# A third late weight set in the first phase, W2 casts ahead of negations, and low parts last in the second layer: a fused attention and expert kernel

## The chip, the cores and the metric

One Trainium2 chip, one core. The metric is the device time of one execution in microseconds (us). The engines are TensorE (PE; its weight loads PEld), VectorE (DVE), ScalarE (ACT), GpSimd (POOL) and SyncE (SP, which issues most DMAs). Each takes its instructions in the order of its own queue, and they wait for one another by semaphores.

## The reference

A linear attention with a complex decay over 768 steps, for 4 batches and 8 heads of 48 dimensions; its output, 3072 tokens of 384 features, goes through four experts of 1024 hidden units, whose outputs are summed with normalised weights. In float32:

```
mag   = sqrt(a_re**2 + a_im**2);  scale = minimum(mag, 0.999) / (mag + 1e-06)
a_re, a_im = a_re * scale, a_im * scale
for t in range(768):
    S_re, S_im = a_re[t]*S_re - a_im[t]*S_im + k[t] x v[t],  a_re[t]*S_im + a_im[t]*S_re
    y[t] = q[t] @ S_re
x = y, tokens by (heads * dims)                     # 3072 x 384
p = probs / (probs.sum(-1) + 1e-09)
out = sum over e of p[:, e] * (relu(x @ w1[e]) @ w2[e])
```

## The kernel before

Each large product keeps its float32 precision by splitting both operands into a high and a low part (names hh and hl, whi and wlo, xha and xla, shi and slo) and summing three matmuls: high by high, high by low, low by high. The high part is a copy by ScalarE into the matmul's own type, the low part the difference, by VectorE. For weights the low part is also made without VectorE: a DMA of GpSimd's queue casts the weights into the high part, ScalarE writes its negative into the low part's slot ("negation"), and a second DMA of GpSimd's queue adds the weights onto it.

**First phase (to line 925).** Twelve blocks g of 256 tokens. For each the decay, q and k are worked out on VectorE and ScalarE, the attention on TensorE (scores sc, L588, masked into scs by VectorE, L593; states G), and its output y goes to DRAM (y_d) and comes back as tokens xa. In between, for the block before, experts 0 and 1 run: eight steps f2 of two 128-wide parts u. `w1_step` makes the first layer's ph (18 matmuls, L234), hh (ScalarE, L244) and hl (VectorE, L245); `w2_step` multiplies hh and hl with the weights' second half, for each u and each of two token halves t: (hh, whi), (hh, wlo), (hl, whi), 12 matmuls on L254, into accumulators po. The order of all this is set by a scheduler, from the order in the program and the dependencies. The 16 weight parts of experts 0 and 1 lie in 16 slots each for high and low.

`check_all` and `late_weights(h)` are called ahead of the last block's steps. `late_weights` prepares a *weight set*: the first-layer weights of four of an expert's eight hidden parts, in the form that the second phase wants. It loads them raw (lw, four DMAs, L736), makes 15 sums and differences (`weight_sums`, lws and lwt, VectorE, L743), splits the 20 resulting 128 x 128 tiles by six copies on ScalarE (lwh, lwt, L749) and six subtractions on VectorE (lwl, lwm, L750), and writes both parts to DRAM (late_d, four DMAs on SP's queue, L753 and L754). lwl and lwm have one buffer each. Before, it is done for the two sets of expert 3.

**Second phase (L927 on).** Experts 2 and 3, over rounds R of 768 tokens, each with two units (h = 0 and 1, one weight set each). A unit takes 20 products of sums of tokens (X, parts xh and xl, by `prep_x` from Z, which is loaded from y_d) by the set's 20 tiles, 3 matmuls each (L935, into the accumulators pb0 to pb4), and the list UNIT says in which order they stand among copies to SN (C, by ScalarE), sums of accumulators (D, by VectorE), the hidden parts (H, L: hid) and *fills* F. A fill is a second-layer part `l2` of the unit before (matmuls on L935 into pob). For a set that is not in DRAM yet, `prep_w` loads the raw weights to free space (ACC, RX, SN), and makes the same sums and splits; a set in late_d is loaded by `fetch_w` straight into the slots (slots 0 to 4 for h = 0 of expert 2, 5 to 9 for h = 1, high and low, and a tile ext). Either way `second_w` takes the second-layer weights by casts (L1018), negations (L1020) and accumulating DMAs (L1022) into the slots 3, 4 or 8, 9. Slots become free as experts 0 and 1 finish on the last block.

What isn't TensorE's work in a unit waits in a list, `side`, in order; a B entry of UNIT takes so many of its items, and casts are taken as soon as they are first. Up to `held["on"]` the scheduler may still move the instructions; from there on they stay as written.

Names in the profile: lw0/lw1 are the two late sets, shi and slo the slots, SN the saved accumulators. L938 is any ScalarE copy of the second phase, L941 and L944 any VectorE sum of it, L947 GpSimd's.

Of the kernel before, what the change touches and what calls it, by code (L numbers as in the profile page):

```python
# [16 lines left out]
HD = H * D  # L17
# [104 lines left out]
def fast_path(ctx, tc, qkP, aP, vP, probsP, w, out, flag):  # L122
# [36 lines left out]
    late_d = [dram.tile([P, 2, len(WORDER) * P], F32, name=f"late_d{h}") for h in range(2)]  # L159
# [88 lines left out]
    def w2_step(f2, hh, hl, po):  # L248
        for u in range(2):
            i = 2 * f2 + u  # L250
            hi, lo = wts[i]
            for t in range(CG):
                for n, (ht, wt) in enumerate(((hh, hi), (hh, lo), (hl, hi))):
                    nc.tensor.matmul(po[t], ht[:, u, t * P:(t + 1) * P], wt[:, HD:],  # L254
                                     start=(i % FE == 0 and n == 0),
                                     stop=(i % FE == FE - 1 and n == 2))
# [28 lines left out]
    with ExitStack() as c1:  # L285
# [446 lines left out]
        def late_weights(h):  # L732
            i = (E1 + 1) * FE + 4 * h
            raw = big.tile([P, 4, NJ, P], F32, tag="A", name=f"lw{h}", bufs=NA)
            for u in range(4):
                nc.sync.dma_start(raw[:, u], w[i + u][:, :HD].rearrange("p (k c) -> p k c", k=NJ))  # L736
            s0, s1, h0 = (tmp(f"lw{nm}{h}").rearrange("p c (n x) -> p (c n) x", x=P) for nm in ("s", "t", "h"))
            l0 = big.tile([P, 12, P], F32, tag="qk", name=f"lwl{h}", bufs=1)
            l1 = big.tile([P, 12, P], F32, tag="K", name=f"lwm{h}", bufs=1)
# [11 lines left out]
            for c, (x, y) in enumerate(((h0, h1), (l0, l1))):  # L751
                d = late_d[h][:, c].rearrange("p (n x) -> p n x", x=P)
                nc.sync.dma_start(d[:, :12], x.bitcast(F32))  # L753
                nc.sync.dma_start(d[:, 12:], y[:, :8].bitcast(F32))  # L754
# [125 lines left out]
        for g in range(1, NG + 1):  # L880
            if g == NG:
                check_all()
                for h in range(2):
                    late_weights(h)
# [26 lines left out]
    with ExitStack() as c2:  # L911
# [141 lines left out]
        def fetch_w(e, h, base):  # L1053
            hi, lo, ext = places(e, h, base)
            for c, x in enumerate((hi, lo)):
                for n in range(3):
                    pin(nc.sync.dma_start(x[n].bitcast(F32), late_d[h][:, c, n * 2 * HD:(n + 1) * 2 * HD]))
                pin(nc.sync.dma_start(ext[:, c * 2 * P:(c + 1) * 2 * P].bitcast(F32), late_d[h][:, c, 6 * HD:]))
# [172 lines left out]
        jobs = [prep_w(E1, h, 5 * h, x[:, :half], y) for h, x, y in ((0, ACC, RX), (1, SN, SN[:, half:half + HD]))]  # L1231
# [3 lines left out]
        for job in jobs:  # L1235
            job[0]()
        side.pop(0)
        side += jobs[0][1] + jobs[0][2] + jobs[0][3] + jobs[1][1] + jobs[1][2]
# [232 lines left out]
```

## Time and profile before

| | |
|---|---|
| time, median of 3 executions | 981.32 us (980.24, 981.32, 983.77) |
| the profiled execution | 983.21 us |
| its span in the profile | 981.5 us |
| mean clock granted to TensorE | 0.994 |
| TensorE busy | 950.4 us of the span, 6717 matmuls |
| VectorE, ScalarE, GpSimd busy | 740.7, 479.2, 163.9 us |
| DMA | 134.32 MB, 137 GB/s over the span |

The span is what lies between the first and the last instruction; the execution's time includes some us around it. The first phase takes the span up to about 600 us, with the two phases overlapping from 564 us, when the first load of Z starts. Times inside the profile are counted from the start of the span. A timeline row gives start, length, engine, line, operation and tiles, with x3 for three of a kind in a row; in brackets stands how long the engine was idle before it, and what that was waiting for. Rows of tables by stretches give the window, then its length and the busy times of PE, PEld, DVE, ACT and POOL, each with the number of instructions, then PEclk, DMA share and GB/s.

### The profile page before, as it was taken

Reading aid. Unit: us, or ns where it says so; the run is one execution under the profiler, and the core shown is the slowest. Engines: PE = TensorE matmul, PEld = TensorE weight load, DVE = VectorE, ACT = ScalarE, POOL = GpSimd, SP = SyncE. Lnnn points to the kernel's source line nnn. Section 1 sums busy time; section 2 is a strip of 40 time slices with the busy share of each in tenths; the row PEclk is TensorE's granted clock in tenths of the full one; section 3 lists DMA queues with packets and bytes.
Section 4 is the critical chain, followed back from the end, with each engine's and each line's share of the span. In section 5 each row is a group of like instructions: output and inputs, shape, how many; then the busy total and the mean of one; then the engine's idle time right before and its main releaser. Section 6 shows DMA issues by size and latency. Waiting matters only on the chain.

```text
span 981.5 us, 17593 instructions
## 1 busy us (share of the span) xinstructions
PE 950.4 (97%) x6717; PEld 924.7 (94%) x6717; DVE 740.7 (75%) x1610; ACT 479.2 (49%) x952; POOL 163.9 (17%) x206
## 2 busy tenths in 40 slices
PE   5899998999999999999999999999999999999997
PEld 3799998999999999999999998999999999999997
DVE  7888989898888889878896286767675857576643
ACT  7755435355363636436263256545453545454430
POOL 6030000000000000000000007333533352323000
PEclk9999999999999999999999999999999999999999
DMA  9585276674756657393769159231513444131112
GB/s 300 182 158 158 57 194 141 158 152 147 175 138 157 157 134 177 123 226 107 169 162 296 49 177 293 57 97 49 137 66 113 162 124 112 49 99 49 49 49 76
DMA packets 110510, 134.32 MB, mean 137 GB/s; under 512 B 7824, under 2 KB 95424, under 8 KB 110416
## 3 DMA queue, kind: packets, MB, share of 16 engines
q1 hardware_dynamic: 98928, 106.17, 38.5%
q0 software_dynamic: 11488, 26.93, 11.7%
q8 instruction: 55, 0.90, 0.4%
q14 instruction: 39, 0.32, 0.1%
HBM read 87.20 MB, written 45.86 MB: 136 GB/s over the span
## 4 chain that ended last, share of the span: by engine, by line
PE 81%; DVE 6%; DMA 6%; ACT 4%; issue 1%; POOL 0%; SPq 0%; DVEq 0%; ACTq 0%; POOLq 0%
PE pob L935 20%; PE ph L234 17%; PE po L254 16%; PE pb L935 16%; PE sc L588 4%; PE dp L574 3%; PE yp L609 2%; PE yp L604 2%; PE ktp L556 1%; DMA y_d<-y 1%; DMA Kst<-k_d 1%; DMA shi<-w 1%; DMA xa<-y_d 1%; DMA wst<-w 1%; PE xp L639 1%
## 5 line engine op out<-in xcount | busy, mean ns | idle before, releaser
L935 PE MATMUL pob<-shi,hid 128*128 128x384 f32 x528 | 148.9, 336 | 0.7 <-DVE hid L944 0.6
L254 PE MATMUL po<-whi,hh 128*128 128x384 f32 x384 | 129.8, 339 | 1.1 <-ACT hh L244 1.1
L254 PE MATMUL po<-wlo,hh 128*128 128x384 f32 x384 | 129.1, 336 | 0.0
L254 PE MATMUL po<-whi,hl 128*128 128x384 f32 x384 | 124.6, 339 | 1.7 <-DVE hl L245 1.6
L244 ACT ACTIVATE hh<-ph 128x512 fp32r<-128x512 f32 x96 | 57.1, 595 | 140.5 <-PE ph L234 136.4
L947 POOL TENSOR_TENSOR Z<-Z 128x384 f32<-128x384 f32 x84 | 90.4, 1118 | 115.0 <-DVE xl L941 50.6
L234 PE MATMUL ph<-xha,whi 128*128 128x256 f32 x576 | 104.0, 287 | 1.2 <-ACT xha L221 1.2
L234 PE MATMUL ph<-xla,whi 128*128 128x256 f32 x576 | 101.1, 284 | 0.4 <-DVE xla L223 0.4
L234 PE MATMUL ph<-xha,wlo 128*128 128x256 f32 x576 | 101.3, 284 | 0.0
L935 PEld LDWEIGHTS pob<-shi,hid 128*128 128x128 f32 x528 | 96.5, 188 | 2.0 <-DVE hid L944 1.2
L935 PE MATMUL pb<-xh,shi 128*128 128x384 f32 x291 | 97.8, 338 | 0.3 <-DVE pb L941 0.2
L935 PE MATMUL pb<-xl,shi 128*128 128x384 f32 x288 | 97.0, 337 | 0.0
L935 PE MATMUL pb<-xh,slo 128*128 128x384 f32 x288 | 97.0, 337 | 0.0
L245 DVE SCALAR_TENSOR_TENSOR hl<-ph,hh 128x512 fp32r<-128x512 f32 x96 | 65.9, 687 | 35.4 <-ACT hh L244 34.8
L935 PE MATMUL pob<-slo,hid 128*128 128x384 f32 x264 | 88.4, 335 | 0.0
L234 PEld LDWEIGHTS ph<-xha,whi 128*128 128x128 f32 x576 | 85.9, 190 | 2.5 <-ACT xha L221 1.5
L234 PEld LDWEIGHTS ph<-xla,whi 128*128 128x128 f32 x576 | 82.6, 191 | 0.6 <-DVE xla L223 0.6
L234 PEld LDWEIGHTS ph<-xha,wlo 128*128 128x128 f32 x576 | 82.8, 190 | 0.2 <-issue 0.2
L938 ACT ACTIVATE SN<-pb 128x384 f32<-128x384 f32 x96 | 47.1, 492 | 65.7 <-PE pb L935 58.2
L941 DVE TENSOR_TENSOR xl<-Z,xh 128x384 fp32r<-128x384 f32 x104 | 59.9, 606 | 21.5 <-ACT xh L938 13.6
L938 ACT ACTIVATE hid<-pb 128x384 fp32r<-128x384 f32 x76 | 37.2, 490 | 75.9 <-PE pb L935 75.5
L254 PEld LDWEIGHTS po<-whi,hl 128*128 128x128 f32 x384 | 70.8, 188 | 3.3 <-DVE hl L245 3.2
(232 smaller groups left out, 2098.5 us busy)
## 6 DMA issues: line engine op xcount, KB each, us to landing
qk<-qkP SPq DMA_DIRECT2D x24, 384.0 KB, 7.1
acc_d<-acc POOLq DMA_DIRECT2D x24, 384.0 KB, 5.1
ACC<-acc_d SPq DMA_DIRECT2D x48, 192.0 KB, 3.2
A<-aP SPq DMA_DIRECT2D x22, 384.0 KB, 8.2
Z<-y_d SPq DMA_DIRECT2D x16, 384.0 KB, 3.8
q_d<-Q SPq DMA_DIRECT2D x12, 387.0 KB, 4.0
Qst<-q_d SPq DMA_DIRECT2D x12, 387.0 KB, 6.0
v<-vP SPq DMA_DIRECT2D x24, 192.0 KB, 2.7
```

The source lines that it names most:

```text
L234: ins = nc.tensor.matmul(ph[:, u, :], wt[:, j * P:(j + 1) * P], xt[:, j, :], start=(n == 0), stop=(n == 3 * NJ - 1))
L244: wts["hh"] = nc.scalar.activation(hh, ph, AF.Relu)
L245: nc.vector.scalar_tensor_tensor(hl, ph, 0.0, hh, op0=ALU.max, op1=ALU.subtract)
L254: nc.tensor.matmul(po[t], ht[:, u, t * P:(t + 1) * P], wt[:, HD:], start=(i % FE == 0 and n == 0), stop=(i % FE == FE - 1 and n == 2))
L574: ins = nc.tensor.matmul(d_ps[:, h, :], KT[:, h, :], vc[:, h * D:(h + 1) * D], start=True, stop=True)
L588: ins = nc.tensor.matmul(s_ps[:, h, :], Kc[:, hf * 4 + h, :], Qc[:, hf * 4 + h, :], start=True, stop=True)
L604: ins = nc.tensor.matmul(yo, st[:, o:o + n], Qc[:, o // D, :], start=True, stop=False)
L609: ins = nc.tensor.matmul(yo, vc[:, o:o + n], sc[h // 4][:, h % 4, :], start=first, stop=True)
L935: return tc.keep_in_program_order(nc.tensor.matmul(*args, **kw))
L938: return pin(nc.scalar.activation(dst, src, fn, scale=scale))
L941: pin(nc.vector.tensor_tensor(dst, x, y, op=op))
L947: nc.gpsimd.tensor_tensor(dst, x, y, op=op)
```

## The change

Four edits:

- `late_weights` is called for three sets, (expert 2, h = 0), (expert 3, h = 0) and (expert 3, h = 1); the first of them is new. The second phase then fetches this set with `fetch_w` and no longer loads, sums and splits it; `prep_w` remains for (expert 2, h = 1).
- In `side` both sets' casts of second-layer weights come first, then the first set's negations, then the sums of the second. The negations of slots 8 and 9 (`late`) come in the first unit behind a gap of four, with one token sum ahead of them.
- `w2_step` takes all eight products of hh first, for both u and t, and then the four of hl.
- In unit 1 the fill that is left empty is the sixth and no longer the eighth.

```diff
--- before.py
+++ after.py
@@ -156,7 +156,8 @@
     y_d = [dram.tile([HD, G], F32, name=f"y_d{g}") for g in range(NG)]
     acc_d = [dram.tile([P, CG, HD], F32, name=f"acc_d{g}") for g in range(NG)]
 
-    late_d = [dram.tile([P, 2, len(WORDER) * P], F32, name=f"late_d{h}") for h in range(2)]
+    late_d = {(e, h): dram.tile([P, 2, len(WORDER) * P], F32, name=f"late_d{e}_{h}")
+              for e, h in ((E1, 0), (E1 + 1, 0), (E1 + 1, 1))}
 
     wts = {}
     whi = {}
@@ -246,14 +247,14 @@
         return hh, hl
 
     def w2_step(f2, hh, hl, po):
-        for u in range(2):
-            i = 2 * f2 + u
-            hi, lo = wts[i]
-            for t in range(CG):
-                for n, (ht, wt) in enumerate(((hh, hi), (hh, lo), (hl, hi))):
-                    nc.tensor.matmul(po[t], ht[:, u, t * P:(t + 1) * P], wt[:, HD:],
-                                     start=(i % FE == 0 and n == 0),
-                                     stop=(i % FE == FE - 1 and n == 2))
+        for part in ((hh, (0, 1)), (hl, (0,))):
+            for u in range(2):
+                i = 2 * f2 + u
+                for t in range(CG):
+                    for n in part[1]:
+                        nc.tensor.matmul(po[t], part[0][:, u, t * P:(t + 1) * P], wts[i][n][:, HD:],
+                                         start=(i % FE == 0 and part[0] is hh and n == 0),
+                                         stop=(i % FE == FE - 1 and part[0] is hl))
 
     class MoE:
         def __init__(self):
@@ -729,14 +730,14 @@
             nc.tensor.matmul(n_ps, good, one1, start=True, stop=True)
             nc.vector.tensor_scalar(flag, n_ps, float(P), None, op0=ALU.is_lt)
 
-        def late_weights(h):
-            i = (E1 + 1) * FE + 4 * h
-            raw = big.tile([P, 4, NJ, P], F32, tag="A", name=f"lw{h}", bufs=NA)
+        def late_weights(e, h):
+            i = e * FE + 4 * h
+            raw = big.tile([P, 4, NJ, P], F32, tag="A", name=f"lw{i}", bufs=NA)
             for u in range(4):
                 nc.sync.dma_start(raw[:, u], w[i + u][:, :HD].rearrange("p (k c) -> p k c", k=NJ))
-            s0, s1, h0 = (tmp(f"lw{nm}{h}").rearrange("p c (n x) -> p (c n) x", x=P) for nm in ("s", "t", "h"))
-            l0 = big.tile([P, 12, P], F32, tag="qk", name=f"lwl{h}", bufs=1)
-            l1 = big.tile([P, 12, P], F32, tag="K", name=f"lwm{h}", bufs=1)
+            s0, s1, h0 = (tmp(f"lw{nm}{i}").rearrange("p c (n x) -> p (c n) x", x=P) for nm in ("s", "t", "h"))
+            l0 = big.tile([P, 12, P], F32, tag="qk", name=f"lwl{i}", bufs=1)
+            l1 = big.tile([P, 12, P], F32, tag="K", name=f"lwm{i}", bufs=1)
             rows, last_ = raw[:, :3], raw[:, 3]
             for ops in weight_sums((s0, s1), rows, last_):
                 for o in ops:
@@ -749,7 +750,7 @@
                 nc.scalar.activation(hi, src, AF.Copy)
                 nc.vector.tensor_tensor(lo, src, hi, op=ALU.subtract)
             for c, (x, y) in enumerate(((h0, h1), (l0, l1))):
-                d = late_d[h][:, c].rearrange("p (n x) -> p n x", x=P)
+                d = late_d[e, h][:, c].rearrange("p (n x) -> p n x", x=P)
                 nc.sync.dma_start(d[:, :12], x.bitcast(F32))
                 nc.sync.dma_start(d[:, 12:], y[:, :8].bitcast(F32))
 
@@ -880,8 +881,8 @@
         for g in range(1, NG + 1):
             if g == NG:
                 check_all()
-                for h in range(2):
-                    late_weights(h)
+                for e, h in late_d:
+                    late_weights(e, h)
             first = FIRST.get(g, 2)
             end = first + len(MORE) - 1
 
@@ -1054,8 +1055,8 @@
             hi, lo, ext = places(e, h, base)
             for c, x in enumerate((hi, lo)):
                 for n in range(3):
-                    pin(nc.sync.dma_start(x[n].bitcast(F32), late_d[h][:, c, n * 2 * HD:(n + 1) * 2 * HD]))
-                pin(nc.sync.dma_start(ext[:, c * 2 * P:(c + 1) * 2 * P].bitcast(F32), late_d[h][:, c, 6 * HD:]))
+                    pin(nc.sync.dma_start(x[n].bitcast(F32), late_d[e, h][:, c, n * 2 * HD:(n + 1) * 2 * HD]))
+                pin(nc.sync.dma_start(ext[:, c * 2 * P:(c + 1) * 2 * P].bitcast(F32), late_d[e, h][:, c, 6 * HD:]))
             ready.add(("w", e, h))
             return second_w(e, h)
 
@@ -1228,14 +1229,14 @@
                     bg(op[1])
 
         half = C2 * HD
-        jobs = [prep_w(E1, h, 5 * h, x[:, :half], y) for h, x, y in ((0, ACC, RX), (1, SN, SN[:, half:half + HD]))]
+        casts, rests = fetch_w(E1, 0, 0)
+        loads, sums, more, late = prep_w(E1, 1, 5, ACC[:, :half], RX)
         freed.update(range(16))
         side += prep_x(0)
         side[0][2]()
-        for job in jobs:
-            job[0]()
+        loads()
         side.pop(0)
-        side += jobs[0][1] + jobs[0][2] + jobs[0][3] + jobs[1][1] + jobs[1][2]
+        side += casts + more + rests + sums
         drain()
         held["on"] = True
         todo_x = []
@@ -1250,8 +1251,8 @@
                     side += todo_x[:1]
                     tail = []
                     if R == 0:
-                        side += [["gap", None, 2, None]] + jobs[1][3] + [["gap", None, 2, None]]
-                    if R in (1, NB2):
+                        side += todo_x[1:2] + [["gap", None, 4, None]] + late
+                    elif R in (1, NB2):
                         casts, tail = fetch_w(E1 + 1, *((0, 10) if R == 1 else (1, 0)))
                         side += todo_x[1:2] + [["gap", None, 3, None]] + casts
                     else:
@@ -1268,7 +1269,7 @@
                 def fill(k, u=2 * R + h):
                     if u == 0 and k == 0:
                         mo.flush()
-                    elif u > 1 or (u, k) == (0, 6) or (u == 1 and k < FE - 1):
+                    elif u > 1 or (u, k) == (0, 6) or (u == 1 and k != 5):
                         l2()
 
                 unit(R, h, fill)
```

Lines of the program behind the first edit are one higher than before: L245 becomes L246, L750 L751, L938 L939, L1018 L1019.

In the rows below, in the order in which an engine takes them, the brackets name whose semaphores a row waits for: an engine, or a DMA queue (DMAHW for SP's, DMASW for GpSimd's).

**VectorE, end of the late sets, ahead of the last block's first scores.** Before (lw1 is the last set, hl10_1 the hidden low part that TensorE's step of block 10 waits for, scs11 masked scores of block 11):

```order
L750 TENSOR_TENSOR lwl1_6535<-lws1_6532,lwh1_6534 128x768 [waits DMAHW4_49,Activation_49]
L750 TENSOR_TENSOR lwm1_6536<-lw1_6527,lwt1_6533 128x256 [waits DMAHW7_49]
L581 TENSOR_TENSOR G11_0_6175<-G10_1_5906,dp11_0_6166 112x384 [waits PE_49]
L750 TENSOR_TENSOR lwm1_6536<-lw1_6527,lwt1_6533 128x128
L750 TENSOR_TENSOR lwm1_6536<-lw1_6527,lwt1_6533 128x256
L750 TENSOR_TENSOR lwm1_6536<-lwt1_6533 128x384
L750 TENSOR_TENSOR lwl1_6535<-lws1_6532,lwh1_6534 128x768 [waits Activation_49]
L245 SCALAR_TENSOR_TENSOR hl10_1_6136<-ph10_1_6116,hh10_1_6135 128x512 [waits Activation_49]
L593 TENSOR_TENSOR scs11_0_0_6182<-sc11_0_0_6177,maskp_140 128x512 [waits PE_49]
L593 TENSOR_TENSOR scs11_0_1_6189<-sc11_0_1_6184,maskp_140 128x512 [waits PE_49]
```

After, the same place, where lw24 and lw28 are the second and the third set:

```order
L751 TENSOR_TENSOR lwl24_6536<-lws24_6533,lwh24_6535 128x768 [waits DMAHW4_49,Activation_49]
L751 TENSOR_TENSOR lwm24_6537<-lw24_6528,lwt24_6534 128x256 [waits DMAHW0_49]
L751 TENSOR_TENSOR lwm24_6537<-lw24_6528,lwt24_6534 128x128
L751 TENSOR_TENSOR lwm24_6537<-lw24_6528,lwt24_6534 128x256
L751 TENSOR_TENSOR lwm24_6537<-lwt24_6534 128x384
L751 TENSOR_TENSOR lwl24_6536<-lws24_6533,lwh24_6535 128x768 [waits Activation_49]
L744 TENSOR_TENSOR lws28_6574<-lw28_6569 128x384 [waits DMAHW7_49,DMAHW2_49,DMAHW1_49]
L744 TENSOR_TENSOR lws28_6574<-lw28_6569 128x128
L744 TENSOR_TENSOR lws28_6574<-lw28_6569 128x128 [waits DMAHW3_49]
L744 TENSOR_TENSOR lws28_6574<-lw28_6569 128x256
L744 TENSOR_TENSOR lws28_6574<-lw28_6569 128x128
L744 TENSOR_TENSOR lwt28_6575<-lw28_6569 128x128 [waits DVE_49]
```
```order
L582 TENSOR_TENSOR G11_0_6176<-G10_1_5907,dp11_0_6167 112x384 [waits PE_49]
L744 TENSOR_TENSOR lwt28_6575<-lw28_6569 128x128 x2
L246 SCALAR_TENSOR_TENSOR hl10_1_6137<-ph10_1_6117,hh10_1_6136 128x512 [waits Activation_49]
L744 TENSOR_TENSOR lws28_6574<-lws28_6574,lw28_6569 128x256 [waits DVE_49]
L744 TENSOR_TENSOR lws28_6574<-lws28_6574 128x256 [waits DVE_49]
L594 TENSOR_TENSOR scs11_0_0_6183<-sc11_0_0_6178,maskp_141 128x512 [waits PE_49]
```

The wait for the first set's write (lwm1, lwm24) stays; behind it six sums of the third set, waiting for its loads, now stand ahead of G11_0, and two more ahead of hl10_1.

**ScalarE, in the first unit.** slo8 and slo9 are negations, SN copies of accumulators, hid hidden parts. Before:

```order
L938 ACTIVATE hid0_7128<-pb3_7115 128x384 [waits PE_49]
L938 ACTIVATE SN_6894<-pb1_7081 128x384 [waits PE_49]
L938 ACTIVATE slo8_6948<-shi8_6943 128x384 [waits DMASW1_49]
L938 ACTIVATE slo8_6948<-shi8_6943 128x384 [waits DMASW2_49]
L938 ACTIVATE slo9_6949<-shi9_6944 128x384 [waits DMASW3_49]
L938 ACTIVATE hid1_7144<-pb4_7118 128x384 [waits PE_49]
L938 ACTIVATE SN_6894<-pb0_7077 128x384 [waits PE_49]
L938 ACTIVATE SN_6894<-pb1_7081 128x384 [waits PE_49]
L938 ACTIVATE slo9_6949<-shi9_6944 128x384 [waits DMASW4_49]
L938 ACTIVATE SN_6894<-pb0_7077 128x384 [waits DVE_49,PE_49]
```

After:

```order
L939 ACTIVATE hid0_7152<-pb3_7139 128x384 [waits PE_49]
L939 ACTIVATE SN_6936<-pb1_7100 128x384 [waits PE_49]
L939 ACTIVATE hid1_7162<-pb4_7142 128x384 [waits PE_49]
L939 ACTIVATE SN_6936<-pb0_7096 128x384 [waits PE_49]
L939 ACTIVATE SN_6936<-pb1_7100 128x384 [waits PE_49]
L939 ACTIVATE SN_6936<-pb0_7096 128x384 [waits DVE_49,PE_49]
L939 ACTIVATE slo8_6998<-shi8_6993 128x384 [waits DMASW4_49]
L939 ACTIVATE slo8_6998<-shi8_6993 128x384 [waits DMASW5_49]
L939 ACTIVATE hid2_7198<-pb3_7139 128x384 [waits PE_49]
L939 ACTIVATE shi15_7206<-SN_6936 128x384 [waits DVE_49]
```

The negations moved from ahead of hid1 and three copies to SN to behind them.

**GpSimd's queue, start of the second phase.** DMA rows with shi are casts, those with slo accumulations. Before:

```order
L1018 DMA shi3_6932<-w 128x384 [waits DMASW1_49,PE_49]
L1018 DMA shi3_6932<-w 128x384
L1018 DMA shi4_6933<-w 128x384 [waits DMASW3_49,PE_49]
L1018 DMA shi4_6933<-w 128x384
L1022 DMA slo3_6937<-w 128x384 [waits DMASW5_49,Activation_49]
L1022 DMA slo3_6937<-w 128x384 [waits Activation_49]
L1022 DMA slo4_6938<-w 128x384 [waits DMASW7_49,Activation_49]
L1022 DMA slo4_6938<-w 128x384 [waits DMASW0_49,Activation_49]
L947 TENSOR_TENSOR Z_6893<-Z_6893 128x384 [waits DMAHW3_49,DMAHW4_49,DMAHW2_49,DMAHW5_49,DMAHW1_49,DMAHW6_49,DMAHW0_49,DMAHW7_49,DVE_49,Pool_49]
L1018 DMA shi8_6943<-w 128x384 [waits DMASW1_49,PE_49]
L1018 DMA shi8_6943<-w 128x384 [waits DMASW2_49]
```

After:

```order
L1019 DMA shi3_6974<-w 128x384 [waits PE_49]
L1019 DMA shi3_6974<-w 128x384 [waits DMASW1_49]
L1019 DMA shi4_6975<-w 128x384 [waits PE_49]
L1019 DMA shi4_6975<-w 128x384 [waits DMASW3_49]
L1019 DMA shi8_6993<-w 128x384 [waits PE_49]
L1019 DMA shi8_6993<-w 128x384 [waits DMASW5_49]
L1023 DMA slo3_6979<-w 128x384 [waits Activation_49]
L1023 DMA slo3_6979<-w 128x384 [waits DMASW7_49,Activation_49]
L1019 DMA shi9_6994<-w 128x384 [waits DMASW0_49,PE_49]
L1019 DMA shi9_6994<-w 128x384 [waits DMASW1_49]
L1023 DMA slo4_6980<-w 128x384 [waits DMASW2_49,Activation_49]
```

The casts of shi8 and shi9 moved ahead of the first token sum (Z), in between those of slo3 and slo4.

## The prediction

> **What bounds the kernel now.** The page's head and its table of busy times come first, then TensorE's waits.
>
> ```profile
> span 981.5 us, 17593 instructions
> PE 950.4 (97%) x6717; PEld 924.7 (94%) x6717; DVE 740.7 (75%) x1610; ACT 479.2 (49%) x952; POOL 163.9 (17%) x206
> ```
> ```profile
> PE lp L202 <- DMA wst<-w: 9.6, 1, 9.6
> PE qp L446 <- DVE Q L486: 2.5, 1, 2.5
> PE pb L935 <- ACT SN L938: 2.1, 1, 2.1
> PE po L254 <- DVE hl L245: 1.6, 3, 0.7
> ...
> PE kp L565 <- ACT KT L557: 0.6, 1, 0.6
> PE pob L935 <- DVE hid L944: 0.6, 1, 0.6
> ```
>
> TensorE works for 950.4 of 981.5 us, so 31.1 us of idling is all that an order can win at an unchanged clock. The change alters no matmul's shape and no count of them, so I look only at where TensorE stops, or runs slowly. In the waits (engine, line, what was waited for: total, times, longest) the first two rows, 12.1 us, are the kernel's start, which the change leaves alone. The four below lie where it moves something.
>
> The three waits of the second layer are these, in TensorE's timeline (start, length, work, in brackets the idle time before and its releaser):
>
> ```profile
> 205.68 0.44 PE L254 MATMUL po<-whi,hl 128*128 128x384 f32 x1 [0.46 <-DVE hl L245]
> 431.12 0.44 PE L254 MATMUL po<-whi,hl 128*128 128x384 f32 x1 [0.42 <-DVE hl L245]
> 576.59 0.62 PE L254 MATMUL po<-whi,hl 128*128 128x384 f32 x2 [0.75 <-DVE hl L245]
> ```
>
> The longest stop of the second phase, and what ScalarE did then:
>
> ```profile
> 610.87 0.62 PE L935 MATMUL pb<-xh,ext 128*128 128x384 f32 x2 [2.07 <-ACT SN L938]
> ```
> ```profile
> 608.02 0.53 ACT L938 ACTIVATE slo<-shi 128x384 fp32r<-128x384 f32 x1 [0.89 <-DMA shi<-w]
> 609.54 0.52 ACT L938 ACTIVATE slo<-shi 128x384 fp32r<-128x384 f32 x1 [0.99 <-DMA shi<-w]
> 609.97 0.47 ACT L938 ACTIVATE hid<-pb 128x384 fp32r<-128x384 f32 x1
> 610.34 0.86 ACT L938 ACTIVATE SN<-pb 128x384 f32<-128x384 f32 x2
> ```
>
> ScalarE takes its instructions in order. Three negations (slo<-shi) stand ahead of hid and the SN copies, and two of them wait for casts of W2 that GpSimd issued only here:
>
> ```profile
> 588.59 2.16 POOL L1018 DMA_DIRECT2D shi<-w  x4
> 600.79 2.22 POOL L1018 DMA_DIRECT2D shi<-w  x4
> ```
>
> The SN copies free the accumulators that TensorE wants next, so it stops for 2.07 us. That is not all it costs. The table by stretches shows the clock right behind the stop (PEclk, the last column but two):
>
> ```profile
> 612.00:613.00 1.00, 1.00 (x5) 0.98 (x4) 0.69 (x2) 0.19 (x1) 0.90 (x2) 0.50 1.09 201
> 613.00:614.00 1.00, 1.00 (x5) 1.00 (x5) 0.55 (x2) 0.49 (x1) 1.00 (x3) 0.50 1.17 202
> 614.00:615.00 1.00, 1.00 (x5) 1.00 (x5) 1.00 (x3) 0.16 (x1) 1.00 (x3) 0.50 1.15 198
> 615.00:616.00 1.00, 1.00 (x6) 1.00 (x5) 0.89 (x3) 0.74 (x2) 0.12 (x1) 0.80 1.15 198
> ```
>
> Three us at half the clock and one at 0.80 lose 3 x 0.5 + 0.2 = 1.7 us. I read this as the price of the stop, so that it goes with the stop.
>
> The Trainium skill, "TensorE: Matmul & The Clock Gate", Part 1, has the gate go to half speed after an idle window of about 3.4 us, in windows that run freely. By that rule a stop of 2.07 us can't do it, and the slow stretch would stay: 1.7 us less gain. The stretch's length, 3 to 4 us, agrees with one such window; what started it does not, and where the two differ I go by the trace.
>
> **The low parts last.** A step of the second layer is 12 matmuls. Before, hl is read by the third of them, now by the ninth, so VectorE gets six matmuls more. What such a place costs, and what follows on it:
>
> ```profile
> 534.75 0.34 PE L254 MATMUL po<-whi,hh 128*128 128x384 f32 x1
> 534.93 0.34 PE L254 MATMUL po<-wlo,hh 128*128 128x384 f32 x1
> ```
>
> They start 0.18 us apart, so six give 1.1 us, more than the longest wait of 0.75. All three go: -1.6 us (0.46 + 0.42 + 0.75). The reordering itself costs nothing, for the same instructions stand in the same step.
>
> The scheduler also rearranges a little around blocks 0 to 1 (82 to 95 us): KT's copies on ScalarE now stand behind a logarithm and an exponential of the next group. The nearest row is the existing wait for KT, 0.6 us: it can go (-0.6), or grow by one or two such activations (+1.5). I take +0.5.
>
> **The transition.** In the changed order the casts of weights 8 and 9 stand in GpSimd's queue right behind those of 3 and 4, ahead of its first Z sum. They start where the last reader of those slots in the first phase ends, not at 600.79:
>
> ```profile
> 591.25 0.34 PE L254 MATMUL po<-whi,hl 128*128 128x384 f32 x1
> ```
>
> The old ones were waited for until 609.5, 8.7 us behind the first issue; from 592 on, the same gives about 601. The negations now stand behind hid1 and the SN copies, and would start near 607. So both causes go: no SN copy stands behind a negation that waits. -2.1 us for the stop, and -1.7 for the clock. Who waits for the later negations: GpSimd's accumulation of slo8 and slo9, then their reads in unit 2, over 10 us on.
>
> The fetched set comes by eight DMAs of 2.6 MB (six of 128 x 768 floats, two of 128 x 256), in place of four raw loads, 15 sums and six splits. Those sums were VectorE's work up to 600, where TensorE does not wait for it, so their absence wins nothing by itself. But two small loads of ext now go ahead of the Z loads on SP's queue, for which VectorE waits already:
>
> ```profile
> 571.62 1.50 DVE L941 TENSOR_TENSOR Z<-Z 128x384 f32<-128x384 f32 x3 [1.49 <-DMA Z<-y_d]
> ...
> 575.85 0.68 DVE L245 SCALAR_TENSOR_TENSOR hl<-ph,hh 128x512 fp32r<-128x512 f32 x1
> ```
> ```profile
> 574.98 0.34 PE L254 MATMUL po<-whi,hh 128*128 128x384 f32 x1
> ```
>
> One subtraction (0.5) has moved from ahead of this hl to behind it, so it would end at 576.0 if Z comes as before, and at 576.9 if Z comes 0.9 us later, two issues. The ninth matmul wants it at 574.98 + 8 x 0.18 = 576.4. I put 0.2 us on this (0 to 0.5).
>
> The wait for hid is 0.60 us:
>
> ```profile
> 635.86 0.62 PE L935 MATMUL pob<-shi,hid 128*128 128x384 f32 x2 [0.60 <-DVE hid L944]
> ```
>
> VectorE's rows there are the same as before, only with less ahead of them. Between 0 and 0.6 I take 0.3.
>
> **The third late set.** What it adds on VectorE is read from the two that are there, the sums by their group (count, busy time) and the end of the second set by the timeline:
>
> ```profile
> L743 DVE TENSOR_TENSOR lws<-lw 128x128 f32<-128x128 f32 (+2 forms) x10 | 3.2, 365 | 0.1
> ```
> ```profile
> 528.90 0.42 DVE L750 TENSOR_TENSOR lwm<-lw,lwt 128x256 fp32r<-128x256 f32 x1 [1.51 <-DMA late_d<-lwm]
> 529.25 0.55 DVE L581 TENSOR_TENSOR G<-G,dp 112x384 f32<-112x384 f32 x1
> ...
> 530.72 0.95 DVE L750 TENSOR_TENSOR lwl<-lws,lwh 128x768 fp32r<-128x768 f32 x1
> 531.59 0.68 DVE L245 SCALAR_TENSOR_TENSOR hl<-ph,hh 128x512 fp32r<-128x512 f32 x1
> ```
>
> The second set's last part starts at 528.90, when the first set's lwm has been written out (its buffer is the only one). Now the first group of subtractions waits for the same write, and behind it stand lwl, six sums of the third set, G11_0 and two more sums, and only then hl10_1. One load of the third set is issued ahead of that write, so I let the wait end at 530.3, 1.4 us later. From there, by these rows: four lwm 1.4 (528.90 to 530.72 without G), lwl 0.9, six sums 1.7 (five are half of the 3.2, one more is about 0.3, and neighbours overlap a little), G11_0 0.5, two sums 0.4, hl 0.7: 535.9. The ninth matmul wants it at 534.75 + 8 x 0.18 = 536.2. So hl10_1 comes just in time; with its third matmul wanting it, at 535.1, it would be 0.8 us late. Of the two masked scores scs11_0 behind it each comes some tenths later than before; between 0 and 2.5 us lie open here, by what these rows can slip, and I take 0.5, since the sum above ends just in time. What speaks for a small price is the empty time behind: in the table by stretches VectorE (third column of busy times) is free from there on, and so are the DMA queues (last column but one).
>
> ```profile
> 520.00:530.00 10.00, 10.00 (x79) 10.00 (x78) 8.38 (x27) 5.65 (x11) 0.85 (x1) 1.00 1.08 329
> 530.00:540.00 10.00, 10.00 (x93) 9.56 (x92) 4.18 (x7) 1.59 (x3) 0.00 (x0) 1.00 0.67 211
> 540.00:550.00 10.00, 10.00 (x94) 9.56 (x93) 2.07 (x3) 3.36 (x9) 0.00 (x0) 1.00 0.12 29
> ```
>
> **The sum.** -1.6 (hl) - 2.1 (stop) - 1.7 (clock) - 0.3 (hid) + 0.5 (block 0 to 1) + 0.2 (Z) + 0.5 (late set) = -4.5 us. The profiled execution took 983.21 us, which gives 978.7; against the median of the three runs, 981.32 (the profiled one is 1.9 above it), 976.8. About 0.5%, 4.9 us, is what a measurement of this kernel can tell from no change, so the forecast lies just at that edge.
>
> **Rivals.**
>
> *Everything gained, nothing paid.* Without the three costs and with the whole of hid: -1.6 - 2.1 - 1.7 - 0.6 = -6.0, 975.3. For it speak VectorE's empty rows behind 530; against it the order of ScalarE at 82 us. Chance 0.2.
>
> *The stop moves.* The copy that TensorE waits for also waits for VectorE in the changed order, and for its own place behind the other work. If another wait holds SN as long, the 2.1 and 1.7 stay: -1.6 - 0.3 + 1.2 = -0.7, 980.6. For it: DMA share is still 1.1 in the rows from 612 to 616, so the casts can land late again. Against it: they are issued 8 to 9 us sooner. Chance 0.2.
>
> *The slow stretch is not the stop's.* Then 1.7 stay: -2.8, 978.5. (The rule of the Trainium skill's "TensorE: Matmul & The Clock Gate", Part 1, told above, gives the same.) For it: the DMA queues are full in the same four rows, so something else than the stop is special there. Against it: it begins 1 us behind the stop's end. Chance 0.1.
>
> *Slower: the late set holds VectorE.* The DMA share was 1.08 already from 520 to 530; the third set adds 0.8 MB of loads and 2.6 MB of writes there, some 10 us of the queues at the 329 GB/s of that row. If the loads land at 540 rather than by 532.6, where the sums are ready for them, the six sums, hl10_1 and scs11 wait in VectorE's queue: hl10_1 would be ready near 543.3, 7 us late, and such a stop would bring a slow stretch (1.7) too. -4.5 - 0.5 + 7.1 + 1.7 = +3.8, 985.1. It decides from a stop of about 3.3 us (3.3 + 1.7 = 5.0), which is loads landing behind 536. Against it: the share falls to 0.67 in the ten us behind. Chance 0.1.
>
> **How the numbers follow.** The forecast has 0.4, with 974.8 to 978.5 as its own range, by the bounds of its costs. Below 976.4 (faster by over 0.5%) lie the first rival and half of the forecast: 0.4. Slower by over 0.5% is the last: 0.1. The rest, 0.5, is within. The range leaves out the last rival and the lowest tail of the first: 974.0 to 982.0.
>
> **What would show it.** The waits list without hl; no stop near 610 and PEclk 1.00 from 608 to 620; in VectorE's timeline the subtraction behind the write near 530, and hl10_1 by 536; TensorE without a stop at 535 to 546; KT's wait near 92. A stop over 3 us between 534 and 548, or one near 610 with another releaser, would make the prediction wrong.

## The result and the profile after

The changed kernel takes 976.15 us (median of 6 executions, 974.47 to 977.94), the kernel before, run beside it, 983.03 (980.24 to 987.04). The ratio is 0.9931, with a 95% interval of 0.9906 to 0.9956: 0.69% faster, 0.44 to 0.94. The profiled execution took 977.62 us with a span of 975.8, which is 5.7 us less than the span of before, where 4.5 was forecast; the medians lie 6.9 us apart.

The head of the page after, and TensorE's waits (engine, line, what was waited for: total, times, longest); each line number is one higher than before:

```profile
span 975.8 us, 17612 instructions
...
PE 946.6 (97%) x6717; PEld 923.2 (95%) x6717; DVE 740.7 (76%) x1610; ACT 479.2 (49%) x952; POOL 165.0 (17%) x206
```
```profile
PE pb L936 <- DVE pb L942: 1.2, 2, 1.0
...
PE po L255 <- DVE hl L246: 0.9, 1, 0.9
PE kp L566 <- ACT KT L558: 0.7, 1, 0.7
PE pob L936 <- DVE hid L945: 0.5, 1, 0.5
```

The row "pb <- ACT SN" is gone. Of the three waits for hl one is left, 0.9 us, and there is a new one of 1.0 for a sum of VectorE. Something does not add up at first: the waits fell by little (TensorE idled for 31.1 us of the span before, for 975.8 - 946.6 = 29.2 now), and still the span is 5.7 us shorter, since the *busy* time fell by 3.8 with the same matmuls: about 1.5 of it is the slow stretch of before, and for the rest see e7 and e8.

Where the time went is seen best by matmuls: the start of the n-th matmul of either trace, set against the n-th of the other. So far ahead is the changed kernel:

| n | before, at us | ahead by, us |
|---|---|---|
| 240 | 51.7 | 0.5 |
| 1440 | 203.0 | 0.1 |
| 1680 | 233.4 | 1.3 |
| 3240 | 426.5 | 1.7 |
| 3960 | 515.5 | 2.4 |
| 4320 | 560.1 | 2.2 |
| 4560 | 595.4 | 2.4 |
| 4680 | 619.3 | 4.9 |
| 4920 | 663.1 | 6.0 |

Behind 663 us nothing moves any more. So 2.4 us come from the first phase, 2.6 from the first unit, where the long stop was, and 1.1 from unit 2 near 634 to 645 (the time axis of before).

GpSimd's queue after, the casts that were at 588.59 and 600.79:

```profile
576.53 1.13 POOL L1019 DMA_DIRECT2D shi<-w  x2 [5.76 <-PE po L255]
580.45 2.13 POOL L1019 DMA_DIRECT2D shi<-w  x4 [2.79 <-PE po L255]
...
584.69 1.23 POOL L1019 DMA_DIRECT2D shi<-w  x2
```

All eight are issued by 586, where the prediction had those of slots 8 and 9 start from 592 on: the slots come free sooner than it read.

ScalarE, then VectorE, then TensorE at the place of the old stop:

```profile
607.49 0.93 ACT L939 ACTIVATE slo<-shi 128x384 fp32r<-128x384 f32 x2
...
610.31 0.92 ACT L939 ACTIVATE slo<-shi 128x384 fp32r<-128x384 f32 x2
611.14 0.47 ACT L939 ACTIVATE slo<-pb 128x384 fp32r<-128x384 f32 x1
```
```profile
611.64 0.56 DVE L945 SCALAR_TENSOR_TENSOR slo<-pb,slo 128x384 fp32r<-128x384 f32 x1 [0.64 <-ACT slo L939]
612.12 0.56 DVE L942 TENSOR_TENSOR pb<-pb,SN 128x384 f32<-128x384 f32 x1
```
```profile
612.73 0.44 PE L936 MATMUL pb<-xh,shi 128*128 128x384 f32 x1 [0.98 <-DVE pb L942]
```

The negations no longer wait for a DMA. But two of them, at 610.31, stand ahead of a copy (slo15) that VectorE waits for, and behind that stands the sum that TensorE needs: the stop is shorter and has another cause. The table by stretches (window; length and busy times of PE, PEld, DVE, ACT, POOL; PEclk; DMA share; GB/s) shows that no slow clock follows it:

```profile
612.00:613.00 1.00, 0.27 (x1) 0.28 (x2) 1.00 (x3) 0.27 (x1) 1.00 (x3) 1.00 0.75 131
613.00:616.00 3.00, 3.00 (x19) 3.00 (x19) 2.17 (x5) 1.84 (x4) 1.52 (x3) 1.00 1.08 225
```

The hl that is still waited for, in VectorE's and TensorE's timeline:

```profile
570.76 1.50 DVE L942 TENSOR_TENSOR Z<-Z 128x384 f32<-128x384 f32 x3 [1.01 <-DMA Z<-y_d]
...
574.52 0.68 DVE L246 SCALAR_TENSOR_TENSOR hl<-ph,hh 128x512 fp32r<-128x512 f32 x1
```
```profile
575.26 0.62 PE L255 MATMUL po<-whi,hl 128*128 128x384 f32 x2 [0.85 <-DVE hl L246]
```

TensorE is here 2.2 us earlier than before, but Z is only 0.9 us earlier (570.76, before 571.62): its loads, and the two of ext now ahead of them, do not follow TensorE's gain. The length of this wait is not fixed: in five executions of this order (the changed kernel, e7, e4, the changed kernel's later run f1, and e8) the starts there lie 1.19, 1.37, 1.06, 0.67 and 0.40 us apart. And the late set, with VectorE's rows and the hl matmuls:

```profile
528.02 0.96 DVE L751 TENSOR_TENSOR lwm<-lw,lwt 128x256 fp32r<-128x256 f32 x3 [3.72 <-DMA late_d<-lwm]
...
530.24 1.49 DVE L744 TENSOR_TENSOR lws<-lw 128x384 f32<-128x384 f32 x5
...
532.72 0.68 DVE L246 SCALAR_TENSOR_TENSOR hl<-ph,hh 128x512 fp32r<-128x512 f32 x1
```
```profile
533.67 0.87 PE L255 MATMUL po<-whi,hl 128*128 128x384 f32 x4
```

hl10_1 is ready at 533.4, 0.3 us before its first reader, as forecast, and the sums did not wait for their loads.

### The profile page after: what moved, and what is told of

It reads as the page before. It is cut to its first block, busy times and chain, and to the rows that moved or that the text cites. A ratio compares the mean times of both kernels' runs of the same rounds, so it can differ in the third digit from the quotient of the medians.

```text
span 975.8 us, 17612 instructions
## 1 busy us (share of the span) xinstructions
PE 946.6 (97%) x6717; PEld 923.2 (95%) x6717; DVE 740.7 (76%) x1610; ACT 479.2 (49%) x952; POOL 165.0 (17%) x206
## 4 chain that ended last, share of the span: by engine, by line
PE 84%; DVE 5%; DMA 4%; ACT 3%; issue 1%; SPq 0%; DVEq 0%; ACTq 0%
PE pob L936 20%; PE ph L235 18%; PE po L255 17%; PE pb L936 16%; PE sc L589 4%; PE dp L575 3%; PE yp L610 2%; PE yp L605 2%; DMA k_d<-K 1%; PE ktp L557 1%; DMA lw<-w 1%; DMA Kst<-k_d 1%; PE xp L640 1%; DVE xl L942 1%; DVE lws L744 1%
## 5 line engine op out<-in xcount | busy, mean ns | idle before, releaser
L245 ACT ACTIVATE hh<-ph 128x512 fp32r<-128x512 f32 x96 | 57.1, 594 | 135.4 <-PE ph L235 134.8
L246 DVE SCALAR_TENSOR_TENSOR hl<-ph,hh 128x512 fp32r<-128x512 f32 x96 | 65.9, 687 | 35.3 <-ACT hh L245 34.6
L255 PE MATMUL po<-whi,hl 128*128 128x384 f32 x384 | 84.9, 337 | 0.9 <-DVE hl L246 0.9
L939 ACT ACTIVATE SN<-pb 128x384 f32<-128x384 f32 x96 | 47.3, 492 | 67.1 <-PE pb L936 59.8
L255 PEld LDWEIGHTS po<-whi,hh 128*128 128x128 f32 x384 | 72.4, 189 | 1.5 <-ACT hh L245 1.5
L939 ACT ACTIVATE hid<-pb 128x384 fp32r<-128x384 f32 x76 | 37.3, 490 | 72.2 <-PE pb L936 71.8
```

The lines of the kernel that those rows point to most:

```text
L245: wts["hh"] = nc.scalar.activation(hh, ph, AF.Relu)
L246: nc.vector.scalar_tensor_tensor(hl, ph, 0.0, hh, op0=ALU.max, op1=ALU.subtract)
L255: nc.tensor.matmul(po[t], part[0][:, u, t * P:(t + 1) * P], wts[i][n][:, HD:], start=(i % FE == 0 and part[0] is hh and n == 0), stop=(i % ...
L939: return pin(nc.scalar.activation(dst, src, fn, scale=scale))
```

## The experiments

All but e7, which was only profiled, were timed against the kernel before on the same chip. "Ahead" is read as in the table above, from the profiled execution.

| run | what it is | median, us | ratio to before (95%) | span, us |
|---|---|---|---|---|
| e1 | before, low parts last | 980.49 | 0.9973 (0.9950 to 0.9995) | 981.1 |
| e3 | before, casts first | 979.27 | 0.9965 (0.9942 to 0.9988) | 977.3 |
| e9 | before, third set made but unused | 982.87 | 1.0000 (0.9985 to 1.0014) | 977.9 |
| e2 | changed, low parts mixed | 978.67 | 0.9967 (0.9956 to 0.9978) | 975.7 |
| e8 | changed, eighth fill empty | 977.24 | 0.9937 (0.9915 to 0.9959) | 975.6 |
| e4 | changed, negations early | 976.20 | 0.9932 (0.9909 to 0.9956) | 975.3 |
| e6 | e4, and Z loaded first | 975.37 | 0.9922 (0.9892 to 0.9952) | 973.4 |
| e10 | before, low last, casts first, negations early | 975.28 | 0.9935 (0.9922 to 0.9948) | 972.7 |
| e11 | e10, sixth fill empty | 974.30 | 0.9910 (0.9886 to 0.9934) | 972.8 |

Spans alone differ by a us or so from one execution to the next, at the start and at the loads of the first phase's scores (L588); so a run's argument rests on its rows, and these are of one execution. That of e1 was the longest of its ten (982.80 us), those of e9 and e10 were the shortest of their ten and six.

**e1, low parts last alone.** `w2_step` of the changed kernel in the kernel before.

```diff
-                for n, (ht, wt) in enumerate(((hh, hi), (hh, lo), (hl, hi))):
+        for part in ((hh, (0, 1)), (hl, (0,))):
```

> The kernel before with the low parts last in the second layer, and nothing else of the change. Theory: hl is wanted six matmuls (1.05 us) later, so the three waits for hl near 205, 431 and 576 us go, and with them the gaps between matmul starts of 0.80, 0.76 and 1.09 us; counted by starts (gap less 0.17, and 0.10 more for the slow start behind it) that is 0.73 + 0.69 + 1.02 = 2.4 us, not the 1.6 that the idle column sums to. Span about 979, the stop near 610 with its slow clock unchanged. Rival: the gain of the first phase is the scheduler's rearrangement or chance, the waits come back at other places of the same blocks: span within 0.8 us of before.

All waits for hl go, and TensorE is 3.1 us ahead at 578 us. But at 616 it is 0.2 ahead. GpSimd, ScalarE and TensorE there:

```profile
597.66 2.37 POOL L1018 DMA_DIRECT2D shi<-w  x4
```
```profile
605.82 0.52 ACT L938 ACTIVATE slo<-shi 128x384 fp32r<-128x384 f32 x1 [2.08 <-DMA shi<-w]
607.33 0.52 ACT L938 ACTIVATE slo<-shi 128x384 fp32r<-128x384 f32 x1 [0.99 <-DMA shi<-w]
608.73 0.52 ACT L938 ACTIVATE slo<-shi 128x384 fp32r<-128x384 f32 x1 [0.88 <-DMA shi<-w]
```
```profile
610.06 1.01 PE L935 MATMUL pb<-xh,ext 128*128 128x384 f32 x2 [4.25 <-ACT SN L938]
```

The casts are issued 3.1 us sooner than before (597.66, before 600.79), but the last of these negations starts only 0.8 us sooner (608.73, before 609.54). So TensorE waits longer for them: 4.25 us, not 2.07, with 6.8 us of slow clock behind it. The theory was right in the first phase and wrong about the stop, which was not "unchanged": in this execution it took the gain back. Why the casts took longer is not shown. By the median of all ten, 1.7 us below that of before, some of the gain stays.

**e3, casts first alone.**

```diff
-        side += jobs[0][1] + jobs[0][2] + jobs[0][3] + jobs[1][1] + jobs[1][2]
+        side += jobs[0][2] + jobs[1][2] + jobs[0][1] + jobs[0][3] + jobs[1][1]
```

> The kernel before, with the casts of slots 8 and 9 issued ahead of all sums and negations of the second phase; the two late sets, the negations' places and the order in the second layer as before. Theory: ScalarE was held by negations that waited for casts; with the casts landed the stop of 2.07 us near 610 falls below 0.6 us and the slow stretch of 3.4 us behind it (1.7 us) goes too: 3.5 to 4 us less from there on, span 977.5 to 978. Rival 1: the stop stays, since SN waits for VectorE's sums of the first set there: span within 1 us of before. Rival 2: the stop goes but the slow stretch stays: 2.3 us less.

```profile
605.70 1.34 ACT L938 ACTIVATE slo<-shi 128x384 fp32r<-128x384 f32 x3
606.94 0.48 ACT L938 ACTIVATE hid<-pb 128x384 fp32r<-128x384 f32 x1
```

The three negations run one behind the other, no wait between them; no stop over 0.5 us is left and no slow clock. Between 605 and 619 us TensorE gains 3.3 us, a little under the 3.5 expected, for a new gap of 0.42 us between starts comes at 613.4. The theory holds in its cause, and both rivals fall.

**e9, the third set alone.** Loaded, summed, split and written in the first phase; nothing reads it.

> The kernel before, with the third late set loaded, summed, split and written in the first phase, and nothing that uses it (the second phase makes its own, as before). Theory: the set lies in VectorE's and the DMA queues' empty time behind 530 and costs little: TensorE 0.5 to 1.7 us later between 524 and 545 (hl10_1 about 0.7, a wait for Kst or scs 0 to 1), and no more; from there the kernel before. Rival, the slower one of the prediction: its loads land late, hl10_1 stops TensorE for 3 us or more and the clock drops.

TensorE loses 0.3 us near 535, under the 0.5 to 1.7 expected, and the ratio is 1.0000. What the set adds is hidden: the slower rival of the prediction falls. The price is not the same each time: in e4's execution TensorE falls 1.5 us behind the changed kernel's here (0.7 us idle for a load of scores and 0.3 for hl), in e2 and e8 it loses nothing. Up to 578 us e9 is 2.2 us ahead of before, although nothing there was changed to its advantage: 1.0 of it is a wait for scores near 263 us that did not come, 1.0 the wait for hl at 576, which is absent here in the old order too. That much moves from one execution to the next. e9 shows something else too: its stop near 608 is nearly as long as that of before, but the clock stays.

```profile
608.20 0.62 PE L936 MATMUL pb<-xh,ext 128*128 128x384 f32 x2 [1.94 <-ACT SN L939]
```
```profile
608.00:611.00 3.00, 2.80 (x16) 2.81 (x17) 2.71 (x6) 1.92 (x5) 2.56 (x5) 1.00 1.12 216
```

**e2, the changed kernel with the old second layer.**

> The changed kernel with the second layer's order of before (hl third, sixth, ninth and twelfth). Theory: the waits for hl come back at 205 and 431 (0.7 us each by starts), the one at 575 grows by 1 us, and a new one of 0.7 us comes at 533, where hl10_1 stands behind the third set's sums: 3 to 3.5 us more than the changed kernel, span 978.5 to 979.5. Rival: waits for the transition's DMAs take up what TensorE loses ahead of them: 1 us more or less.

Inconclusive. The median is 2.5 us above the changed kernel's, where 3 to 3.5 were expected, and the two were not timed on one chip. In the profiled execution the wait at 205 us came back (0.5 us idle) and those at 431 and 533 did not; at 533 TensorE came 0.7 us later than in the changed kernel and hl was ready. The wait at 575 did not grow but shrank, to 0.2 us idle. Its span is the changed kernel's.

**e8, the fill.**

```diff
-                    elif u > 1 or (u, k) == (0, 6) or (u == 1 and k != 5):
+                    elif u > 1 or (u, k) == (0, 6) or (u == 1 and k < FE - 1):
```

> The changed kernel with the eighth fill of unit 1 left empty, as before. Theory: 1.0 us more from unit 2 on, the waits for hid of before come back. Rival: no difference, within 0.3 us; what went there in the changed kernel was then VectorE's, from the first set's sums.

TensorE loses 1.1 us between 628 and 639: matmul starts 0.39, 0.93, 0.40, 0.31 and 0.42 us apart, as before, where the changed kernel has 0.23, 0.25 and 0.87. The theory holds: this gain is the fill's. It is there in every profiled run with the sixth fill empty and in none with the eighth.

**e4 and e6, the two stops of the changed kernel.** e4:

```diff
-        side += casts + more + rests + sums
+        side += casts + more + rests + late + sums
...
-                        side += todo_x[1:2] + [["gap", None, 4, None]] + late
+                        side += todo_x[1:2]
```

> The changed kernel with the negations of slots 8 and 9 moved ahead of the first unit (behind the first set's negations), where ScalarE is idle and their casts have landed. Theory: the stop near 612.7 us of the changed kernel (matmul starts 1.32 us apart, waiting for a VectorE sum behind slo15, which ScalarE made late behind two negations) goes: 1.25 us less from there on. Rival: the negations hold hh or the splits of slots 5 and 6 in ScalarE's queue near 590 and the first unit starts later: no gain or up to 1 us lost.

The stop at 612.7 goes but for a gap of 0.42 us between starts, and TensorE gains 0.9 us there, where 1.25 was expected. The time does not show it (ratio 0.9932, the changed kernel's 0.9931); the profiled execution lost 1.5 at the late set. In e6 `prep_x(0)` and its loads stand ahead of `fetch_w`:

> As the run before, and the four loads of Z issued ahead of the two small loads of ext on SP's queue. Theory: Z lands some 0.8 us sooner, so the wait for hl near 575 us (matmul starts 1.19 us apart in the changed kernel) goes: 1.1 us less, together with the negations 2.3 us less than the changed kernel. Rival: that wait is set by what VectorE has ahead of hl, not by Z; it stays within 0.3 us, and the sum is that of the run before.

TensorE gains 1.2 us at 575 and 0.9 at 612; no wait for hl is left in its list. The negations' part holds in the rows. Z's part fits but is not shown: e8, with ext ahead of Z, has no idle time there either, only a gap of 0.40 us between starts. What speaks for it is that of the profiles with the low parts last none of the five without ext ahead of Z (e1, e6, e10, e11 and e11's later run f2) has idle time there, and all five with it have at least that gap. In time e6 can't be told from the changed kernel (0.9922, the changed one 0.9931).

**e10 and e11, without the third set.**

```diff
+        side += jobs[0][2] + jobs[1][2] + jobs[0][1] + jobs[0][3] + jobs[1][3] + jobs[1][1]
```

> The kernel before with three of the edits and no third late set: low parts last, all casts first, and the negations of slots 8 and 9 behind those of 3 and 4, ahead of the second set's sums. Theory: the third set is not what wins; the waits for hl (2.4 to 3.1 us by starts), the stop near 610 (2.3) and the slow stretch (1.7) all go without it: span 974.5 to 976, as the changed kernel or up to 1 us less. Rival: without the third set VectorE's sums and splits of the first set near 580 to 600 hold the negations or the first unit, once TensorE comes there 3 us sooner: a new stop of 1 to 3 us near 600, span 977 to 979.

```diff
-                    elif u > 1 or (u, k) == (0, 6) or (u == 1 and k < FE - 1):
+                    elif u > 1 or (u, k) == (0, 6) or (u == 1 and k != 5):
```

> The kernel of e10 (two late sets, low parts last, casts first, negations early) with the changed kernel's empty fill of unit 1 (the sixth, not the eighth). Theory: the waits for hid in unit 2 (matmul starts 0.39, 0.94, 0.40, 0.31 and 0.42 us apart near 630 us) shrink to those of the changed kernel (0.23, 0.25, 0.87): 1.0 us less than e10, span near 971.7, time near 974, about 2 us less than the changed kernel. Rival: the waits come from the work in VectorE's queue and move with it: within 0.3 us of e10.

e10 is 8.8 us ahead of before at 820 us, with no wait for hl and only the gap of 0.42 us in the first unit; its span is below the range expected, its time (0.9935) that of the changed kernel. So the third set is not what wins. e11's waits for hid near 630 shrank as in e8's comparison and TensorE gained 1.1 us there; its span is not shorter than e10's, for it lost 1.2 at two loads of scores (L588) at 304 and 347 us. The last two runs set e11 and the changed kernel side by side on one chip:

> The changed kernel again, on the chip of the next run, so that the two can be set side by side. Theory (the third late set is not needed): 1.5 to 2.5 us above the next run's median. Rival: the difference seen on two chips was theirs; the medians lie within 0.7 us.

> The kernel of e11 again (two late sets; low parts last, casts first, negations early, sixth fill empty). Theory: 1.5 to 2.5 us below the changed kernel's median, since its waits for hl at 575 (1.1 us) and for the sum behind slo15 at 612.7 (1.25 us) are gone. Rival: within 0.7 us of it.

The changed kernel: 976.69 us (975.29 to 978.91, ratio 0.9935, 0.9916 to 0.9955). e11's kernel: 974.35 (973.26 to 976.35, ratio 0.9919, 0.9899 to 0.9940). The medians are 2.3 us apart, as expected, though one execution of the six overlaps: it beats both kernels, the changed one by 0.2%. This is not the price of the third set alone: the two kernels differ in the place of the negations too, which gives 0.9 us in e4 with the set kept, and set against e6 (0.9922), which has the set, the same negations and Z first, e11's lead (0.9910) lies within the intervals.

**e7, what a stop costs.** The changed kernel with a ScalarE copy repeated in units 4 to 14, so that TensorE stops for 11 different times.

> The changed kernel with one ScalarE copy of the second phase repeated 6 to 17 times more in units 4 to 14 (the same values again), so that TensorE stops in each for a different time, about 0.3 us to 4.5 us. Theory: a stop costs more than its idle time by a fixed 0.25 to 0.3 us (0.17 us of a matmul's modelled end, and 0.10 us of a slower next start), and the clock falls to half for 3.4 us behind some stops from about 2 us on, not behind those under 1.3 us. Rival, by the Trainium skill, "TensorE: Matmul & The Clock Gate", Part 1: only stops of over 3.4 us bring the half clock, and the cost is the idle time alone.

The shortest stop, with the matmuls around it, and the two on either side of the clock's fall:

```profile
696.87 0.34 PE L937 MATMUL pb<-xl,shi 128*128 128x384 f32 x1
698.33 0.45 PE L937 MATMUL pb<-xh,shi 128*128 128x384 f32 x1 [1.11 <-ACT SN L940]
698.61 0.34 PE L937 MATMUL pb<-xh,slo 128*128 128x384 f32 x1
```
```profile
748.49 0.44 PE L937 MATMUL pb<-xh,shi 128*128 128x384 f32 x1 [2.16 <-ACT SN L940]
774.38 0.44 PE L937 MATMUL pb<-xh,shi 128*128 128x384 f32 x1 [2.74 <-ACT SN L940]
```
```profile
748.50:751.50 3.00, 3.00 (x17) 3.00 (x18) 2.49 (x5) 0.95 (x3) 0.00 (x0) 1.00 0.02 5
775.50:778.50 3.00, 3.00 (x12) 3.00 (x11) 2.47 (x6) 0.97 (x3) 0.00 (x0) 0.50 0.00 0
```

Against the changed kernel TensorE falls behind by 1.39 us at the first, where the idle column says 1.11: starts are 1.46 apart in place of 0.17, and the next 0.28 in place of 0.17. The second and third cost 1.97 and 2.43 (idle 1.69 and 2.16). So a stop costs its idle time and 0.28 us, up to 2.16 us of it. The fourth cost 4.59 for 2.74 idle: 0.28, and 1.6 for a slow stretch. That part of the theory holds, and the rival falls on both counts, for 2.74 us of idling brought the slow clock and no stop cost its idle time alone (the second count is the rival's own and not the Trainium skill's). A threshold in us does not hold, since 2.16 us here and 1.94 in e9 brought no slow clock while 2.07 did in the kernel before.

## Why the prediction was right, and where it was not

The sign, the range and the main causes were right; the sizes were not, and the sum came near by luck as much as by them. By places, the forecast had 0.4 us from the first phase, 3.8 from the first unit and 0.3 from unit 2; the rows show 2.4, 2.6 and 1.1. The whole, 6.0 us, is the number of the first rival, "everything gained, nothing paid", but not its account, since two prices were paid, at Z and at 612.7. Two more things went against the text. It gave a gain of over 0.5% a chance of 0.4 and no visible change 0.5. And it named a stop near 610 with another releaser as a sign that it is wrong: there is one, 0.98 us at 612.73 behind a sum of VectorE.

- **Low parts last, -1.6 us.** The mechanism held, the size did not. The term summed idle times, and a stop costs 0.28 us more than its idle time: three stops are 2.4, and 2.4 is what e1 gains at the three places. In the changed kernel a wait of 0.85 us came back at the third, so its first phase has only some 1.3 us from this edit; 0.5 of its 2.4 were gained before 43 us, as in e9, which doesn't have the edit, and for the rest no single row can be named.
- **Z, +0.2.** This is why it stayed, and the term was too small: 1.1 us in the profiled execution, 0.2 to 1.3 in the others of this order. The reckoning put hl and its reader on one time axis as if both moved together; TensorE came 2.2 us sooner and Z only 0.9.
- **The stop, -2.1, and the clock, -1.7.** Right in cause, by e3. 2.6 us were won where 3.8 were forecast: the stop was worth 2.35, the slow stretch 1.5, and the new stop at 612.7 gave 1.25 back. It is what the rival "the stop moves" asked about, at a third of its price, with another releaser: the moved negations themselves, ahead of slo15. The prediction asked whether they would wait, not what they would hold up; e4, which moves them away, removes the stop.
- **The slow stretch is the stop's.** It went with the stop in e3, in e10 and in the changed kernel. The rival in which it had another cause falls (the rule of the Trainium skill's "TensorE: Matmul & The Clock Gate", Part 1, that stood beside it, is taken up at the end).
- **The wait for hid, -0.3.** 1.1 us were won near 634 to 645, and not by what the text gave as a reason, less work ahead on VectorE: e8 shows that it is the fourth edit, the fill, to which the prediction gave no term. Its row of 0.60 us idle is one of five waits there, and the other four (0.39, 0.40, 0.31 and 0.42 us between starts in place of 0.17) hardly show in the idle column, since a matmul's modelled end lies 0.34 us behind its start.
- **The late set, +0.5.** Measured 0.3 to 0.4 (e9, and the changed kernel at 535), nothing (e2, e8) to 2.0 (e4, from 515 to 545 us) in others, and hl10_1 came 0.3 us before its reader, as worked out. The slower rival had its place right and did not come about.
- **Blocks 0 to 1, +0.5.** Between 78 and 98 us less than 0.1 us was lost.

What the change does not need is the third set itself: e10 wins as much without it, and e11 more. Its part in the profiled execution is a cost of 0.3 in the first phase and of 1.1 at Z, and both move from one execution to the next. Not settled is why TensorE's waits at the loads of scores (L588 and L589, near 43, 263, 306, 347 and 526 us) differ by up to 1.0 us each between executions.

## What to carry to other kernels

Cost a stop of the bound engine by the starts around it, not by its idle time, and look for gaps too short for the idle column. When a stop is set by a transfer, what is gained ahead of it can be lost in it: e1 lost its gain, while e9 kept what it had. So look when the transfer lands, not only when it is issued. When an instruction is moved to where it no longer waits, ask what stands behind it there.

## What was not expected of the hardware

The slow clock goes by windows, not by the length of a stop alone. In the trace's record of the clock every slow stretch behind a stop lasts 3.41 us or 6.83, twice that, and the stretches of the kernel before begin at 28.3 and 612.0 us, 171.0 times 3.413 apart. If time is cut into such windows, counted from the run's slow stretches, the share of a window in which TensorE stood (counted from the last start and 0.17 us) decides, in these stops between full-width matmuls:

```
run     stop ends  share of one window idle   slow clock behind it
after   612.73     0.34                       no
e9      608.20     0.32 and 0.30              no
e7      698.33     0.38                       no
e7      723.17     0.54                       no
e7      748.49     0.59                       no
before  610.87     0.66                       3.41 us
e7      774.38     0.68                       3.41 us
e1      610.06     0.70, then 0.60            6.83 us
e7      861.03     1.00, then 0.06            3.41 us
e7      830.83     0.81, then 0.21            6.83 us
```

The five other stops of e7, and the stop near 612 in e2, e8 and the last run of the changed kernel, fit too. So in these runs a window that was idle for 0.66 or more brought a window at half the clock, and 0.59 did not; a second one followed if TensorE stood for 0.21 or more of the first slow one, and not at 0.06. Where the stop falls in the grid decides: the 1.94 us of e9 fell across a border. The rule was read from these stops afterwards; no run was made to test it. The Trainium skill, "TensorE: Matmul & The Clock Gate", Part 1, has windows of 3413 ns that run freely, with which the record agrees, and the half clock after a window that is idle, a gap of over about 3.4 us; here stops of 2.07 and 2.74 us were enough, and the measurement decides. Not covered: in the changed kernel's last run a gap of 1.29 us between starts at 347.5 us, among the attention's narrow matmuls, was followed by 3.41 us of slow clock, at a share of 0.33; how narrow matmuls count was not tried. And not every share below 1 in that record slows a matmul: in e1's execution it stands at 0.949 from 31 to 806 us, but for the slow stretch, while from 663 us on TensorE's starts keep the pace of before to within 0.1 us.
